# Column pieces for the gate and value products of the last three MLP steps of an attention-and-MLP kernel

## The chip, the cores and the metric

The kernel runs as one program on one core of a Trainium2 chip. The core has five engines that run their own instruction streams: TensorE (PE, with its weight loads shown apart as PEld), VectorE (DVE), ScalarE (ACT), GpSimd (POOL) and SyncE (SP, which only issues transfers). The metric is the device time of one execution in microseconds (us); lower is better. The median of three runs of the kernel before is 574.12 us.

## The reference

A gated linear recurrence over 768 tokens (4 batches, 8 heads of 48) gives `y`; its heads side by side are the 3072 x 384 input of a gated MLP with 1536 hidden units.

```python
for t in range(S):
    state = alpha[:, :, t, :, None] * state + np.einsum('bhd,bhe->bhde', k[:, :, t], v[:, :, t])
    y[:, :, t] = np.einsum('bhd,bhde->bhe', q[:, :, t], state)
...
g = x @ w_gate
silu = g * (1.0 / (1.0 + np.exp(-g)))
val = x @ w_val
return (silu * val @ w_out).astype(np.float32)
```

## The kernel before

The recurrence is done in 16 units of 192 tokens (chunks of 64), with short matmuls, scans and transposes. Their result, transposed and split in a high and a low part, is the tile `xT`: 128 partitions of features (three groups `kt` of 128) by 384 tokens. The MLP is done in 96 steps: 8 blocks of 384 tokens, and in each block 12 slices `f` of 128 hidden units. A step `s` has these instructions:

- `g{s}` on TensorE: the gate product, into one tile in PSUM (tag `gps`, one buffer). Operands are split in a high and a low part of type float32r, and three of the four products of parts are taken (`HL`), for each of three `kt`: nine pairs of a weight load of 128 columns and a matmul over 384 tokens, accumulated.
- `v{s}` on TensorE: the value product, in the same way (tag `vps`, one buffer).
- `sl{s}` on ScalarE: SiLU of the whole gate tile into `h`, one instruction; `h{s}` on VectorE: `h` times the whole value tile, one instruction.
- `hh{s}` on ScalarE and `hl{s}` on VectorE or GpSimd: the high part of `h`, and what is left.
- `o{s}` on TensorE: the output product, nine pairs as well, into three tiles `ops0` to `ops2` that gather over the steps of a block.

At the end of the last block, `ot95.0` to `ot95.2` copy the three output tiles on ScalarE, and `os95.0` to `os95.2` store them.

The order of all instructions on each engine is written out by hand in the string `ORDER` (`t` is TensorE, `v` VectorE, `s` ScalarE, `g` GpSimd, `y` SyncE); it holds for the whole main path. The end of it:

```python
... t:g92 s:hh91 t:v92 g:hl91 s:sl92 t:g93 v:h92 s:hh92 g:hl92 t:v93 s:sl93 t:g94 v:h93 t:v94
s:sl94 t:g95 v:h94 t:o91 t:o92 s:hh93 v:hl93 s:sl95 t:v95 s:hh94 g:hl94 t:o93 v:h95 t:o94 s:hh95
v:hl95 t:o95 s:ot95.0 s:ot95.1 y:os95.0 s:ot95.2 y:os95.1 s:os95.2
```

A small matmul `cps` (L931) of a range check stands in this stretch too, ahead of `g93`. Because each PSUM tag has one buffer, `g{s+1}` waits for `sl{s}`, and `v{s+1}` for `h{s}`. `product` (L720 and on) is what the change edits; L725 is its matmul, L757 the one of `out_product`. After the main path a flag decides whether a general path runs; with these inputs it does not.

Of the kernel before, what the change touches and what calls it, by code (L numbers as in the profile page):

```python
# [18 lines left out]
P = 128  # L19
# [3 lines left out]
NB = 384  # L23
# [15 lines left out]
LOW3 = 7.49 / 2.0 ** 32  # L39
F_LEAST = 3.4332275390625e-05  # L40
F_MOST = 122880.0

# [138 lines left out]
def main_path(ctx, tc, q, k, v, alpha, w_gate, w_val, w_out, out, flag, spill):  # L183
# [5 lines left out]
    nc = tc.nc  # L189
# [4 lines left out]
    KT = DM // P  # L194
    NF = DFF // P
# [89 lines left out]
    wsp, groups, wtiles = {}, [], []  # L285
# [84 lines left out]
    for x, t_ in enumerate(sels):  # L370
        nc.gpsimd.memset(t_.bitcast(F32), 0.0)
        for r in (0, BO):
            c0 = SEL + (D if (r > 0) != (x > 0) else 0)
# [302 lines left out]
    xT = {}  # L676
# [39 lines left out]
    HL = ((0, 0), (0, 1), (1, 0))  # L716
# [2 lines left out]

    def product(kind, blk, f):  # L720
        pt = acc[kind, blk, f] = ps.tile([P, NB], F32, tag=kind + "ps", name=f"{kind}{blk}_{f}")
        n = 0
        for kt in range(KT):
            for a, b_ in HL:
                nc.tensor.matmul(  # L725
                    pt, wsp[kind, f][a][:, kt * P : (kt + 1) * P], xT[blk][:, b_, kt, :],
                    start=(n == 0), stop=(n == 3 * KT - 1),
                )
                n += 1

    def silu(blk, f):
        h = acc["h", blk, f] = p2.tile([P, NB], F32, tag="h", name=f"h{blk}_{f}", bufs=NH)
# [150 lines left out]
    def named_step(s):  # L883
        blk, f, first, last = steps[s]
        b = (blk, f)
        todo[f"g{s}"] = lambda eng: product("g", *b)
        todo[f"sl{s}"] = lambda eng: silu(*b)
        todo[f"v{s}"] = lambda eng: product("v", *b)
        todo[f"h{s}"] = lambda eng: hidden(*b)
        todo[f"hh{s}"] = lambda eng: hidden_hi(*b)  # L890
        todo[f"hl{s}"] = lambda eng: hidden_lo(*b, eng)
        todo[f"o{s}"] = lambda eng: out_product(blk, f, first, last)
        for i in range(NTT):

            todo[f"pl{s}.{i}"] = lambda eng, i=i: part_load(blk, i)
            todo[f"ot{s}.{i}"] = lambda eng, i=i: out_rows(blk, f, i, eng)
            todo[f"os{s}.{i}"] = lambda eng, i=i: out_store(blk, f, i, eng)
# [38 lines left out]
def general_path(ctx, tc, q, k, v, alpha, w_gate, w_val, w_out, out, scratch):  # L936
# [73 lines left out]
    with tc.tile_pool(name="hp", bufs=2) as hp, tc.tile_pool(name="hps", bufs=1, space=PSUM) as hps:  # L1010

        def weights(dst, w, rows, cols):
# [8 lines left out]
            for step in single(nc, raw, t):  # L1021
# [7 lines left out]
            nc.vector.tensor_scalar(  # L1029
                out=m, in0=ab, scalar1=F_MOST, scalar2=3.0e38, op0=ALU.is_ge, op1=ALU.mult  # L1030
            )
# [84 lines left out]
```

## Time and profile before

| what | value |
|---|---|
| runs | 571.64, 574.12, 575.03 us; median 574.12 us |
| span of the profiled execution, first to last instruction | 570.8 us (its own device time is not listed apart from the runs; the fastest run is 0.8 us above the span, the median 3.3 us) |
| busy: PE, PEld, DVE, ACT, POOL | 545.7, 527.4, 391.7, 280.5, 134.0 us |
| stretch from the start of `g93` to the end of the last matmul | about 546.7 to 564.2 us |
| after the last matmul | about 6.6 us: one copy, one store |

A row of a timeline gives the start and the duration in us, then engine, line, operation, tiles and forms; `xN` at its end means that N instructions in a row are merged, from the start of the first to the end of the last. PE and PEld are pipelined: one matmul is shown as 0.34 us long while the next starts 0.17 us after it, so a pace is worked out from starts, not from durations.

### The profile page before, as it was taken

What the parts mean: (1) busy time and instruction counts of PE and PEld (TensorE: products, weight loads), DVE (VectorE), ACT (ScalarE), POOL (GpSimd) and SP (SyncE); (2) the same over time, 40 slices, a digit from 0 to 9 for tenths busy, and PEclk for the clock granted to TensorE, in tenths of its full rate; (3) what the DMA queues carried; (4) which work ended last, traced back from release to release, by engine and by line L of the source; (5) the groups of instructions that cost most, each with busy time, mean ns of one, the idle gap of its engine ahead of it and who ended that gap; (6) DMA issues with size and microseconds to landing.
All of it is one profiled execution on the core that took longest, in us unless ns stands there. A gap on an engine that the chain in (4) does not pass through costs nothing.

```text
span 570.8 us, 13758 instructions
## 1 busy us (share of the span) xinstructions
PE 545.7 (96%) x5510; PEld 527.4 (92%) x5510; DVE 391.7 (69%) x601; ACT 280.5 (49%) x621; POOL 134.0 (23%) x152
## 2 busy tenths in 40 slices
PE   4779999999999999999999999999999999999995
PEld 3669889999999999998999999999999999999995
DVE  6899998989989999889889698951793111210211
ACT  6778565325221223232224647675665666655712
POOL 4004513634431320341220022300131121012010
PEclk9989999999999999999999999999999999999998
DMA  7998934314555554554447667753742443324101
GB/s 204 309 318 254 277 82 112 115 40 108 131 146 146 135 132 107 124 126 113 93 100 187 172 156 205 191 141 89 218 111 85 116 132 86 97 73 121 41 2 47
DMA packets 95367, 77.66 MB, mean 136 GB/s; under 512 B 32832, under 2 KB 92224, under 8 KB 95296
## 3 DMA queue, kind: packets, MB, share of 16 engines
q1 hardware_dynamic: 95152, 76.51, 50.2%
q8 instruction: 45, 0.74, 0.6%
q14 instruction: 26, 0.21, 0.1%
q10 hardware_dynamic: 144, 0.20, 0.1%
HBM read 62.52 MB, written 5.90 MB: 120 GB/s over the span
## 4 chain that ended last, share of the span: by engine, by line
PE 76%; DMA 10%; DVE 7%; SPq 3%; issue 2%; ACT 1%; DVEq 0%; ACTq 0%
PE ops L757 24%; PE v L725 23%; PE g L725 22%; DMA raw<-in_moe_w_out_dram 3%; DMA raw<-in_moe_w_gate_dram 2%; PE y L652 2%; PE A L580 2%; PE s L556 2%; DMA raw<-in_moe_w_val_dram 1%; DMA L<-in_k_dram 1%; DMA Le<-in_q_dram 1%; DVE K L531 1%; SPq L436 1%; PE y L635 1%; DVE t L165 1%
## 5 line engine op out<-in xcount | busy, mean ns | idle before, releaser
L725 PE MATMUL v<-xT,w 128*128 128x384 f32 x864 | 166.9, 337 | 3.2 <-DVE h L737 2.4
L725 PE MATMUL g<-xT,w 128*128 128x384 f32 x864 | 167.3, 337 | 0.4 <-ACT h L733 0.4
L757 PE MATMUL ops<-w,hh 128*128 128x384 f32 x576 | 159.8, 338 | 0.0
L725 PEld LDWEIGHTS v<-xT,w 128*128 128x128 f32 x864 | 150.7, 188 | 5.8 <-DVE h L737 3.4
L725 PEld LDWEIGHTS g<-xT,w 128*128 128x128 f32 x864 | 150.7, 188 | 1.4 <-ACT h L733 0.7
L737 DVE TENSOR_TENSOR h<-h,v 128x384 f32<-128x384 f32 x96 | 52.9, 551 | 120.1 <-PE v L725 92.5
L746 POOL TENSOR_TENSOR hl<-h,hh 128x384 fp32r<-128x384 f32 x57 | 65.5, 1150 | 264.7 <-ACT hh L741 263.5
L741 ACT CAST hh<-h 128x384 fp32r<-128x384 f32 x96 | 49.1, 511 | 128.1 <-DVE h L737 70.9
L757 PEld LDWEIGHTS ops<-w,hh 128*128 128x128 f32 x576 | 105.5, 188 | 1.0
L757 PE MATMUL ops<-w,hl 128*128 128x384 f32 x288 | 96.8, 336 | 0.0
L733 ACT ACTIVATE h<-g 128x384 f32<-128x384 f32 x96 | 46.9, 489 | 80.6 <-PE g L725 68.8
L531 DVE STREAM_TRANSPOSE K<-Gs 32x384 f32<-32x384 f32 x96 | 54.7, 570 | 2.3 <-PE A L580 0.4
L757 PEld LDWEIGHTS ops<-w,hl 128*128 128x128 f32 x288 | 54.1, 188 | 0.1
L746 DVE TENSOR_TENSOR hl<-h,hh 128x384 fp32r<-128x384 f32 x39 | 22.9, 589 | 14.8 <-ACT hh L741 14.6
L590 DVE TENSOR_TENSOR X<-s,mask 64x384 f32<-64x384 f32 (+1 forms) x48 | 26.3, 552 | 8.5 <-PE s L556 7.6
L471 DVE TENSOR_TENSOR_SCAN AT<-AT,back 128x771 f32<-128x771 f32 x16 | 30.9, 1933 | 0.6
L462 DVE TENSOR_TENSOR_SCAN Gs<-AT,inj 128x772 f32<-128x772 f32 x16 | 28.7, 1794 | 0.1
L417 PE MATMUL pt<-ident,wide 128*128 128x128 f32 x72 | 14.9, 376 | 11.4 <-POOL mask L243 5.1
L417 PEld LDWEIGHTS pt<-ident,wide 128*128 128x128 f32 x72 | 12.1, 197 | 13.4 <-ACT wide L405 5.1
L319 ACT ACTIVATE wc<-wc,wbias 128x384 f32<-128x384 f32 x36 | 23.4, 650 | 1.2
L318 ACT ACTIVATE wc<-wc,wbias 128x384 f32<-128x384 f32 x36 | 23.3, 648 | 1.2
L839 POOL TENSOR_TENSOR Gs<-trk,Gs 128x768 f32<-128x768 f32 x10 | 17.9, 1785 | 25.3 <-DVE Gs L462 13.8
(118 smaller groups left out, 608.4 us busy)
## 6 DMA issues: line engine op xcount, KB each, us to landing
xT<-X SPq DMA_DIRECT2D x84, 72.0 KB, 2.2
raw<-in_moe_w_gate_dram SPq DMA_DIRECT2D x12, 384.0 KB, 7.5
V<-in_v_dram SPq DMA_DIRECT2D x96, 48.0 KB, 2.8
raw<-in_moe_w_val_dram SPq DMA_DIRECT2D x12, 384.0 KB, 7.9
raw<-in_moe_w_out_dram SPq DMA_DIRECT2D x12, 384.0 KB, 7.5
wc<-in_moe_w_gate_dram SPq DMA_DIRECT2D x12, 384.0 KB, 4.8
wc<-in_moe_w_val_dram SPq DMA_DIRECT2D x12, 384.0 KB, 3.5
wc<-in_moe_w_out_dram SPq DMA_DIRECT2D x12, 384.0 KB, 3.4
```

Of the source, the lines that this page charges most:

```text
L319: nc.scalar.activation(dev, dev, AF.Relu, bias=wbias[:, 1:2], accum_out=wviol[:, 0, i : i + 1])
L417: nc.tensor.transpose(pt[:, j - js.start, :], Wd.rearrange("p j e c -> p (j e c)")[:, j * P : (j + 1) * P], ident)
L462: nc.vector.tensor_tensor_scan(*(x.rearrange("p g t -> p (g t)")[:, ::-1] for x in (Gs, AT, inj)), 0.0, op0=ALU.mult, op1=ALU.add)
L471: nc.vector.tensor_tensor_scan(Af, Af, back[:, 1 : n + 1], back[:, 0:1], op0=ALU.mult, op1=ALU.add)
L531: nc.vector.transpose(out=bass.AP(k0.tensor, k0.offset, [k0.ap[0], (G * 2 * D, NU), (2 * D, G), (1, 32)]), in_=Kg[j * BO + x : j * BO + x ...
L590: nc.vector.tensor_tensor(out=X[r, z, f * GF : (f + 1) * GF, :].rearrange("r g (c t) -> r g c t", c=NU), in0=sps[f][r].rearrange("r g (c t ...
L725: nc.tensor.matmul(pt, wsp[kind, f][a][:, kt * P : (kt + 1) * P], xT[blk][:, b_, kt, :], start=(n == 0), stop=(n == 3 * KT - 1),)
L733: nc.scalar.activation(h, acc.pop(("g", blk, f)), AF.Silu)
L737: nc.vector.tensor_tensor(out=h, in0=h, in1=acc.pop(("v", blk, f)), op=ALU.mult)
L741: nc.scalar.copy(out=hh, in_=acc["h", blk, f])
L746: eng.tensor_tensor(out=hl, in0=acc.pop(("h", blk, f)), in1=hh.bitcast(F32), op=ALU.subtract)
L757: nc.tensor.matmul(ops[blk][i], h[b_][:, i * P : (i + 1) * P], wsp["o", f][a], start=(first and n == 0), stop=(last and n == 2),)
```

## The change

Steps 93, 94 and 95 (block 7, slices 9, 10 and 11) issue their gate and value products in two pieces of columns (tokens): 256 and 128, 320 and 64, 128 and 256. Each piece goes through all nine pairs of weights before the next piece starts, into its own columns of the same PSUM tile, and every pair loads its weights anew. SiLU, the product `h` and all that follows stay single instructions over 384 columns, and `ORDER` is the same.

```diff
+PARTS = {93: (0, 256, 384), 94: (0, 320, 384), 95: (0, 128, 384)}
...
     def product(kind, blk, f):
         pt = acc[kind, blk, f] = ps.tile([P, NB], F32, tag=kind + "ps", name=f"{kind}{blk}_{f}")
-        n = 0
-        for kt in range(KT):
-            for a, b_ in HL:
-                nc.tensor.matmul(
-                    pt, wsp[kind, f][a][:, kt * P : (kt + 1) * P], xT[blk][:, b_, kt, :],
-                    start=(n == 0), stop=(n == 3 * KT - 1),
-                )
-                n += 1
+        cuts = PARTS.get(blk * NF + f, (0, NB))
+        for c0, c1 in zip(cuts, cuts[1:]):
+            n = 0
+            for kt in range(KT):
+                for a, b_ in HL:
+                    nc.tensor.matmul(
+                        pt[:, c0:c1], wsp[kind, f][a][:, kt * P : (kt + 1) * P], xT[blk][:, b_, kt, c0:c1],
+                        start=(n == 0), stop=(n == 3 * KT - 1),
+                    )
+                    n += 1
```

TensorE before, from the range check's matmul to the first output product that follows (`g_9` is the gate tile of slice 9 in block 7, so of step 93; the last number of a name is its buffer's; each row of a product is nine pairs):

```order
L931 MATMUL cps<-oka,ones 1x1
L725 MATMUL g_9_6689<-xT_5746,w_1380 128x384 x9
L725 MATMUL v_9_6704<-xT_5746,w_1533 128x384 x9
L725 MATMUL g_10_6716<-xT_5746,w_1732 128x384 x9
L725 MATMUL v_10_6727<-xT_5746,w_1732 128x384 x9
L725 MATMUL g_11_6739<-xT_5746,w_1874 128x384 x9
L757 MATMUL ops_0_0_6462<-w_1380,hh_7_6673 128x384
```

The same place with the change (lines are four further down):

```order
L935 MATMUL cps<-oka,ones 1x1
L729 MATMUL g_9_6689<-xT_5746,w_1380 128x256 x9
L729 MATMUL g_9_6689<-xT_5746,w_1380 128x128 x9
L729 MATMUL v_9_6713<-xT_5746,w_1533 128x256 x9
L729 MATMUL v_9_6713<-xT_5746,w_1533 128x128 x9
L729 MATMUL g_10_6734<-xT_5746,w_1732 128x320 x9
L729 MATMUL g_10_6734<-xT_5746,w_1732 128x64 x9
L729 MATMUL v_10_6754<-xT_5746,w_1732 128x320 x9
L729 MATMUL v_10_6754<-xT_5746,w_1732 128x64 x9
L729 MATMUL g_11_6775<-xT_5746,w_1874 128x128 x9
L729 MATMUL g_11_6775<-xT_5746,w_1874 128x256 x9
L761 MATMUL ops_0_0_6462<-w_1380,hh_7_6673 128x384
```

Nothing has changed places; five rows of nine pairs have become ten. The last value product, `v95`, stands between the output products `o92` and `o93` on TensorE, before:

```order
L757 MATMUL ops_2_0_6464<-w_1533,hh_8_6700 128x384
L757 MATMUL ops_2_0_6464<-w_1533,hl_8_6702 128x384
L757 MATMUL ops_2_0_6464<-w_1533,hh_8_6700 128x384
L725 MATMUL v_11_6774<-xT_5746,w_1890 128x384 x9
L757 MATMUL ops_0_0_6462<-w_1874,hh_9_6768 128x384
```

and with the change:

```order
L761 MATMUL ops_2_0_6464<-w_1533,hh_8_6709 128x384
L761 MATMUL ops_2_0_6464<-w_1533,hl_8_6711 128x384
L761 MATMUL ops_2_0_6464<-w_1533,hh_8_6709 128x384
L729 MATMUL v_11_6819<-xT_5746,w_1890 128x128 x9
L729 MATMUL v_11_6819<-xT_5746,w_1890 128x256 x9
L761 MATMUL ops_0_0_6462<-w_1874,hh_9_6813 128x384
```

It has become two rows and stands where it stood. On the other four engines the main path has the same instructions in the same order. In all, 54 pairs of a weight load and a matmul of 384 columns have become 108 pairs of 64 to 320 columns.

## The prediction

> **What bounds the kernel now.** I read the page first: its busy table, its slices and its costliest groups.
>
> ```profile
> span 570.8 us, 13758 instructions
> ...
> PE 545.7 (96%) x5510; PEld 527.4 (92%) x5510; DVE 391.7 (69%) x601; ACT 280.5 (49%) x621; POOL 134.0 (23%) x152
> ...
> PEclk9989999999999999999999999999999999999998
> ...
> L725 PE MATMUL v<-xT,w 128*128 128x384 f32 x864 | 166.9, 337 | 3.2 <-DVE h L737 2.4
> L725 PE MATMUL g<-xT,w 128*128 128x384 f32 x864 | 167.3, 337 | 0.4 <-ACT h L733 0.4
> ```
>
> TensorE is busy for 96% of the span, and the two products that the change edits waited 3.2 and 0.4 us in the whole run. But a share over the span says little about the last 18 us, where the edit lies. So next the chain of work that ended last, asked for the end of the run only, and the busy time of that stretch:
>
> ```profile
> 546.65 0.12 PE cps L931 x2
> 546.76 1.77 PE g L725 x9
> 548.53 1.57 PE v L725 x9
> 550.11 1.57 PE g L725 x9
> 551.68 1.57 PE v L725 x9
> 553.25 1.57 PE g L725 x9
> 554.82 3.12 PE ops L757 x18
> 557.95 1.56 PE v L725 x9
> 559.50 4.70 PE ops L757 x27
> ...
> 564.28 0.48 ACT ot L769
> ```
>
> ```profile
> 546.60:564.20 17.60, 17.59 (x102) 17.24 (x101) 3.39 (x7) 4.42 (x9) 2.02 (x2) 1.00 0.01 3
> ```
>
> From `g93` at 546.76 to the last matmul at 564.2 us the chain is TensorE and nothing else: no other engine, no transfer. The columns of the second row are the window, its length, and the busy time of PE, PEld, DVE, ACT and POOL, then the granted clock (1.00: full) and the DMA share. PE and PEld fill the stretch, the other three are idle for three quarters of it or more. So any time that TensorE gains or loses in the six edited products goes to the end one to one.
>
> **What the six products cost now.** Five of the six pieces of the chain are 1.56 or 1.57 us for nine pairs, 0.174 us a pair; the first `g93` has 0.2 us more for what it waits behind the small `cps`, which stays. So 54 pairs cost 54 x 0.174 = 9.4 us.
>
> **What the change removes, adds and moves.** It removes 54 pairs of 384 columns and adds 54 pairs of the wider piece (36 of 256 columns, 18 of 320) and 54 of the narrower (36 of 128, 18 of 64). The columns are as many as before; the weight loads double. It moves nothing and adds no wait: the first matmul of a product waits for its PSUM tile as before, and SiLU and `h` wait for the last piece. The one-buffer PSUM tiles do not bind either:
>
> ```profile
> 548.63 0.49 ACT L733 ACTIVATE h<-g 128x384 f32<-128x384 f32 x1 [0.77 <-PE g L725]
> 549.77 1.59 PEld L725 LDWEIGHTS g<-xT,w 128*128 128x128 f32 x9
> 549.95 1.73 PE L725 MATMUL g<-xT,w 128*128 128x384 f32 x9
> ```
>
> SiLU of step 93 has emptied the gate tile at 549.12, and `g94` starts to fill it at 549.95 (its weights load from 549.77): 0.83 us of slack, and slower products widen it, since `v93` lies between them. Behind `v95` nothing is edited: `h95`, `hh95`, `hl95` and `o93` to `o95` follow its end as they do now. So the sum is one price list: what a pair costs at 256, 320, 128 and 64 columns. No row of this trace has a float32r product of that width, so I bound each from rows.
>
> *The wider pieces.* If a pair costs in proportion to its columns, 0.174 x 256/384 = 0.116 us and 0.174 x 320/384 = 0.145 us; the other end is that it does not shrink at all, 0.174. I take the proportional ends, provided that the weight load keeps up, which is the next question.
>
> *The narrower pieces.* In proportion these would be 0.058 and 0.029 us. A pair can't be faster than its weight load, and what that takes is hidden in the steady stream, where loads simply follow the matmuls. It shows where TensorE starts after a pause:
>
> ```profile
> 93.38 0.30 PEld L725 LDWEIGHTS v<-xT,w 128*128 128x128 f32 x2 [0.77 <-DVE h L737]
> 93.38 0.45 PE L725 MATMUL v<-xT,w 128*128 128x384 f32 x1 [0.45 <-DVE h L737]
> ...
> L725 PEld LDWEIGHTS g<-xT,w x864: 186/188/192, 51.6 to 554.3; 128*128 128x128 f32 x173
> L725 PE MATMUL g<-xT,w x864: 331/335/446, 51.7 to 554.5; 128*128 128x384 f32 x173
> ```
>
> The first row merges two loads: 0.30 us in all, of which the second takes its 0.188 (the row's median), so it started 0.11 us after the first, with nothing in front of it. The second row says the same by another road: the first matmul after the pause is shown as 0.45 us long where the median is 0.335, so it stood 0.11 us before its weights were in. I read both as the time to fill the array with 128 float32r columns: 0.11 us. That is less than the 0.116 of the 256-column piece, so loads stay hidden there, and more than what 128 or 64 columns take to stream. Loads are one ahead at most (in the rows of `g94` the first load starts 0.18 us, one pair, ahead of its matmul), so a run of nine narrow pairs goes at the pace of the loads: 0.11 us a pair at 128 columns and the same at 64. The bounds: 0.058 and 0.029 below, if loads somehow overlap each other; 0.22 above, if such narrow products are paid as full float32 ones (a rival below).
>
> **The sum.**
> - 256 and 128 columns (four products, 36 pairs of each): 0.116 + 0.110 - 0.174 = 0.052 us; x 36 = 1.9 us.
> - 320 and 64 columns (two products, 18 pairs of each): 0.145 + 0.110 - 0.174 = 0.081 us; x 18 = 1.5 us.
> - Together 3.4 us (3.33 before rounding), all on the path. Nothing covers it, and nothing comes back: the 6.6 us behind the last matmul are a copy and a store that don't change.
>
> The page's span of 570.8 becomes 574.2 us. The runs lie above their span (571.64 at the least, 574.12 in the median, 3.3 above this profiled one), so I add the 3.4 us to the median: 577.5 us, 0.6% slower.
>
> [...]
>
> **The rivals.**
>
> *Loads hidden, no loss (the other side: not slower).* If the weight loads of narrow pairs ran ahead by more than one, TensorE would only see columns, which are as many as before: 0 us, 574.1. It decides from the point where two loads overlap so far that a pair falls under 0.058 us. For it: a plain float32 load of the same 128 columns is spaced closer than float32r's, 0.20 - 0.14 = 0.06 us:
>
> ```profile
> 50.64 0.20 PEld L417 LDWEIGHTS pt<-ident,wide 128*128 128x128 f32 x2
> L417 PEld LDWEIGHTS pt<-ident,wide x72: 138/230/231, 5.0 to 51.1; 128*128 128x128 f32 x72
> ```
>
> Against it: that is another type, and the products themselves show 0.11. [...]
>
> *Narrow products paid as full float32.* The width might decide the mode: a float32r product too narrow might go as slowly as a float32 one. What that costs is in the trace:
>
> ```profile
> 20.65 0.82 PE L417 MATMUL pt<-ident,wide 128*128 128x128 f32 x6
> L417 PE MATMUL pt<-ident,wide x72: 271/421/477, 5.1 to 51.2; 128*128 128x128 f32 x72
> L556 PE MATMUL s<-X,Gs 48*64 48x64 f32 x768 | 15.4, 227 | 1.4 <-ACT K L520 1.4
> ```
>
> Six float32 passes over 128 columns start (0.82 - 0.27)/5 = 0.11 us apart, and a float32 product needs two passes: the code issues 16 x 24 = 384 score matmuls at L556, and the row has 768. So 0.22 us at 128 columns; at 64, two loads of 0.06 or two passes of 0.055, 0.12 us. Sum: 36 x (0.116 + 0.22 - 0.174) + 18 x (0.145 + 0.12 - 0.174) = 5.8 + 1.6 = 7.5 us, 581.6. Against it: the built program has one matmul for each pair of a narrow piece, as for a wide one (it has one for a float32 product too, though, so this says little). [...]
>
> *A flat price.* If 0.174 us were the cycle of a load and its matmul whatever the width (a load is shown as 0.188 us long), the 54 added pairs would cost 54 x 0.174 = 9.4 us: 583.5. Against it is the same 0.11 between loads.
>
> **How the numbers follow.** Narrow pairs at the pace of loads: 0.64, around 577.5 with its own range 575.5 to 579.5 (0.10 to 0.12 us a narrow pair moves it by 0.5 us each way, and the three runs before spread by 3.4 us). Paid as float32: 0.20, near 581.6. Hidden: 0.11, near 574.1 or, half way, 576. Flat: 0.05, near 583.5. The range 574.4 to 582.5 leaves out the flat price and half of the hidden case. About 0.5%, 2.9 us, is what a measurement of this kernel can tell from no change. The likeliest case is only just over that, so I give 0.43 of its 0.64 to slower and 0.21 to same; with 0.20 and 0.05 slower is 0.68, same is 0.21 and 0.09 of the hidden case, 0.30, and faster the rest, 0.02.
>
> **What would show it.** In the changed kernel's timeline, runs of nine pairs on PEld of the edited products: by my prices 1.04 us for 256 columns, 1.3 for 320 and 1.0 for both 128 and 64, from first start to the next piece's first start. Nine 64-column pairs as long as nine 128-column ones would show the loads as the limit; half as long, the columns; 128 at twice the length of 64, or x18 instead of x9, the float32 price; 1.57 for each, the flat price. TensorE should still have no wait in that stretch, and the chain should still be TensorE up to the last copy. I am wrong if loads speed up once matmuls are short, if a switch between widths costs something of its own, or if the median moves by its own spread.

## The result, and the profile after

The changed kernel takes 578.21 us in the median of 9 runs (576.82 to 580.04), the kernel before 573.08 us (9 runs, 571.64 to 575.03). The ratio is 1.0089 with a 95% interval of 1.0071 to 1.0107: 5.1 us slower, where 3.4 us were forecast. The profiled execution has a span of 575.1 us where before had 570.8; its own time was 576.82 us, so 1.7 us lie around a span.

The chain of work that ended last, for the end of the changed kernel's run (start, duration, what; lines are four further down than before):

```profile
547.06 0.12 PE cps L935 x2
547.18 2.21 PE g L729 x18
549.39 2.04 PE v L729 x18
551.43 2.30 PE g L729 x18
553.72 2.33 PE v L729 x18
556.05 2.13 PE g L729 x18
558.17 3.13 PE ops L761 x18
561.30 2.03 PE v L729 x18
563.34 4.70 PE ops L761 x27
...
568.11 0.48 ACT ot L773
```

Against the rows of before, the two products of step 93 went from 1.77 and 1.57 to 2.21 and 2.04, those of 94 from 1.57 and 1.57 to 2.30 and 2.33, those of 95 from 1.57 and 1.56 to 2.13 and 2.03. The sum is 9.61 before and 13.04 after: 3.4 us, and the chain from `g93` to the last matmul grew by as much, from 17.45 (546.76 to 564.21) to 20.85 us (547.18 to 568.03). Nothing else is in it. The busy times of that stretch say the same (window, length, then PE, PEld, DVE, ACT, POOL, granted clock):

```profile
547.05:568.03 20.98, 20.97 (x156) 20.62 (x155) 3.39 (x7) 4.42 (x9) 2.02 (x2) 1.00 0.01 2
```

DVE, ACT and POOL do to the hundredth what they did before, and wait for TensorE: in this window `h` on DVE waited 13.9 us in all for the value products, SiLU on ACT 5.1 us for the gate products, and `hl` on POOL 16.2 us for `hh` of ACT, which itself waited 8.6 us for output products. How a pair of each width is paced shows in the timeline of weight loads, cut inside one piece at a time. These are loads of the 64-column, the 128-column, the 320-column and the 256-column pieces, in this order:

```profile
552.75 0.86 PEld L729 LDWEIGHTS g<-xT,w 128*128 128x128 f32 x7
550.42 0.86 PEld L729 LDWEIGHTS v<-xT,w 128*128 128x128 f32 x7
551.61 0.92 PEld L729 LDWEIGHTS g<-xT,w 128*128 128x128 f32 x6
549.64 0.64 PEld L729 LDWEIGHTS v<-xT,w 128*128 128x128 f32 x5
```

With 0.188 us for the last load of each row, the spacing is (0.86 - 0.19)/6 = 0.112 us for 64 columns and the same for 128; 0.92 gives 0.146 for 320, 0.64 gives 0.113 for 256. Half the columns are no faster: the loads set the pace there. At 256 columns the price by columns (0.116) and the load (0.112) lie too close together to tell which of them sets it.

So 3.4 us of the 5.1 are as forecast, and some 1.7 us lie elsewhere. In this profile 0.4 us lie ahead of `g93` (547.18 against 546.76), and another place shows at once: the copy that ends the chain starts 6.5 us before the end of the span before (564.28 of 570.8) and 7.0 us after (568.11 of 575.1). What SyncE waited for there, before and then after (engine and line, releaser: total, times, longest):

```profile
SPq L1084 <- SPq L1084: 3.4, 1, 3.4
```

```profile
SPq L1088 <- SPq L1088: 4.8, 2, 2.9
```

L1084 (now L1088) is the branch around the general path. SyncE stood still on nothing but itself, once before and twice after, in the closing instructions that follow the jump. The page's row on queue 14 has one more transfer of instructions, before and then after:

```profile
q14 instruction: 26, 0.21, 0.1%
```

```profile
q14 instruction: 27, 0.22, 0.1%
```

In the trace's records the second pause is 1.8 us long, from 571.65 to 573.48 us. The view of transfers in just that window has two packets, both on queue 14 (one more, on queue 8, where the page counts 46 and before 45, starts just ahead of that window, at 571.62 us, and takes 0.9 us); in the kernel before two run as well behind its one pause (568.9 to 570.8 us), and SyncE goes on through them. The changed kernel first, then the kernel before:

```profile
q14 instruction: 2, 0.02, 2.8%
```

```profile
q14 instruction: 2, 0.02, 3.2%
```

The 27th transfer starts behind the second pause, at 574.1 us. A wait for data is ruled out: the instruction behind the pause waits for a semaphore that a transfer last raised at 522.1 us (521 to 531 us in the nine profiles below and here that have such a pause).

### The profile page after: what moved, and what is told of

Read it like the earlier page. It is cut to its first block, busy times and chain, and to the rows that moved or that the text cites. A ratio compares the mean times of both kernels' runs of the same rounds, so it can differ in the third digit from the quotient of the medians.

```text
span 575.1 us, 13866 instructions
## 1 busy us (share of the span) xinstructions
PE 545.7 (95%) x5564; PEld 527.6 (92%) x5564; DVE 391.6 (68%) x601; ACT 280.5 (49%) x621; POOL 133.1 (23%) x152
## 4 chain that ended last, share of the span: by engine, by line
PE 77%; DMA 8%; DVE 7%; SPq 4%; issue 2%; ACT 1%; POOL 0%; DVEq 0%; ACTq 0%; POOLq 0%
PE ops L761 23%; PE v L729 23%; PE g L729 22%; DMA L<-in_alpha_dram 2%; PE A L582 2%; PE y L654 2%; PE s L558 2%; SPq L711 2%; DMA raw<-in_moe_w_val_dram 1%; DMA L<-in_k_dram 1%; DMA V<-in_v_dram 1%; PE y L637 1%; PE y L638 1%; DVE K L533 1%; DMA Le<-in_q_dram 1%
## 5 line engine op out<-in xcount | busy, mean ns | idle before, releaser
L729 PE MATMUL v<-xT,w 128*128 128x384 f32 (+3 forms) x891 | 168.5, 333 | 4.5 <-DVE h L741 3.6
L729 PE MATMUL g<-xT,w 128*128 128x384 f32 (+3 forms) x891 | 169.0, 334 | 0.4 <-ACT h L737 0.4
L729 PEld LDWEIGHTS v<-xT,w 128*128 128x128 f32 x891 | 152.7, 188 | 6.8 <-DVE h L741 4.3
L729 PEld LDWEIGHTS g<-xT,w 128*128 128x128 f32 x891 | 152.7, 188 | 1.4 <-ACT h L737 0.7
L419 PE MATMUL pt<-ident,wide 128*128 128x128 f32 x72 | 12.4, 327 | 12.2 <-POOL mask L245 5.1
L419 PEld LDWEIGHTS pt<-ident,wide 128*128 128x128 f32 x72 | 9.9, 168 | 14.0 <-ACT wide L407 5.1
```

Source lines behind the costliest of these rows:

```text
L729: nc.tensor.matmul(pt[:, c0:c1], wsp[kind, f][a][:, kt * P : (kt + 1) * P], xT[blk][:, b_, kt, c0:c1], start=(n == 0), stop=(n == 3 * KT - 1),
```

## The experiments

Two questions: whether it is the loads that price a narrow pair, and what the rest of the loss is. In the accounts, "stretch" is from the chain's first `g93` row to the end of its last output product (17.45 before), and "closing" from the start of the chain's last copy to the end of the span (6.5 us before); the expectations count the closing from the last matmul's start, 0.4 us more. All kernels ran in five rounds beside the kernel before.

**The kernel before, again** (no edit).

> The kernel before, against itself. If the 1.7 us by which the measured loss (5.1 us) exceeds what TensorE's chain lost in the trace (3.4 us) is scatter between executions, two sets of runs of one kernel differ by something of that order, and this ratio lies between 0.998 and 1.002 with an interval of about 0.2% each way. A second profile also shows how far the start of g93 (546.7 us) and the end behind the last matmul (6.6 us) move by themselves: by 0.5 us or more if they are scatter, by under 0.1 us if the 0.4 and 0.5 us seen there belong to the change.

Ratio 0.9996 (0.9980 to 1.0012). Its `cps` ran 0.5 us later than in the first profile, but the stretch and the closing are the same: 564.80 of 571.3, 6.5 us, with one self-wait of 3.2 us. So the 0.4 us ahead of `g93` is within scatter, and the closing hardly moves. That scatter is wide: in the profiles below without an edit ahead of it, `g93` starts anywhere from 546.4 to 550.2 us. Totals are therefore compared by medians, and the closing by its own rows.

**The changed kernel, again** (no edit).

> The changed kernel once more. Loads as the limit: from g93 to the last matmul again 20.85 us in the trace where before had 17.44. The total: 1.006 to 1.007 if only TensorE's 3.4 to 3.9 us count and the first measurement was high by scatter; 1.009 again if there is a constant loss of 1.2 to 1.7 us beside the chain.

Ratio 1.0112 (1.0088 to 1.0136). The stretch is as in the first profile, and the closing is 8.5 us, 567.42 of 575.9. SyncE's waits:

```profile
SPq L1088 <- SPq L1088: 5.2, 2, 3.4
```

The second pause costs 1.8 us (5.2 - 3.4). In the first profile most of it was hidden: SyncE issued its two last stores in 0.85 us, where the kernel before took 1.66, and the first pause was 2.9 us instead of 3.4, together 1.3 us less. Its stores before, and then after:

```profile
563.69 1.66 SPq L774 DMA_DIRECT2D out_dram<-ot  x2
```

```profile
567.52 0.85 SPq L778 DMA_DIRECT2D out_dram<-ot  x2
```

There is a constant loss beside the chain. By the ratio it would be 3.0 us here (6.4 of 573.0, less 3.4), more than the pause; the interval reaches down to 1.6, and whether the rest is more than scatter is not shown.

**The pieces in the middle of the run.**

```diff
-PARTS = {93: (0, 256, 384), 94: (0, 320, 384), 95: (0, 128, 384)}
+PARTS = {57: (0, 256, 384), 58: (0, 320, 384), 59: (0, 128, 384)}
```

> The same pieces in steps 57 to 59, some 220 us from the end, instead of 93 to 95. Loads as the limit: each product's pace is as in steps 93 to 95, the six products lose 3.4 us, and since TensorE waits nowhere for more than 0.5 us after 267 us, the total loses the same 3.4 us (1.006). A loss that belongs to the end of the program (its last instructions, their fetch) would not be there: total 1.006 where the changed kernel has 1.009. If other engines' waits absorb it in the middle, under 1.004.

Ratio 1.0095 (1.0067 to 1.0122). The edited products in the chain:

```profile
369.73 1.98 PE g L729 x18
371.70 1.63 PE ops L761 x9
373.34 1.97 PE v L729 x18
375.31 2.29 PE g L729 x18
377.61 1.67 PE ops L761 x9
379.27 2.24 PE v L729 x18
...
384.98 2.04 PE g L729 x18
387.02 2.07 PE v L729 x18
```

The six take 12.59 us, 3.2 us more than six products of 1.56; the two output products behind narrow pieces take 0.16 us more than the usual 1.57 each, which makes 3.4. The stretch at the end is as in the kernel before (551.84 to 569.28 us, 17.44). So nothing absorbed the loss later, and the place in the run does not matter. The total did not drop to 1.006, and the closing, where nothing was edited, is 9.1 us (569.36 of 578.5):

```profile
SPq L1088 <- SPq L1088: 6.2, 2, 4.2
```

The constant loss has no need of an edit near the end.

**Pieces that alternate within each pair of weights.**

```diff
-        for c0, c1 in zip(cuts, cuts[1:]):
-            n = 0
-            for kt in range(KT):
-                for a, b_ in HL:
+        n = 0
+        for kt in range(KT):
+            for a, b_ in HL:
+                for c0, c1 in zip(cuts, cuts[1:]):
...
-                        start=(n == 0), stop=(n == 3 * KT - 1),
+                        start=(n == 0 and c0 == 0), stop=(n == 3 * KT - 1 and c1 == NB),
...
-                    n += 1
+                n += 1
```

> Same pieces and steps, but the two pieces alternate within each pair of weights (256, 128, 256, 128, ...) instead of nine of one and nine of the other: 17 changes of width in a product instead of 1. Loads as the limit, each one ahead at most: a pair still costs the longer of its columns and the next load, 0.116 + 0.112, so the stretch loses 3.4 us again. A cost of the change of width: 17 times that of one, well over 10 us. Loads that can run further ahead: the wide matmuls hide part of the narrow ones' loads, and the stretch loses under 2 us.

Ratio 1.0120 (1.0089 to 1.0151). The stretch is 20.97 us (546.52 to 567.49), 3.5 us more than before, so seventeen changes of width cost hardly more than one (20.85). Whether loads run further ahead only the products of 320 and 64 columns can tell: 18 loads of 0.112 are 2.02 us, about what a product of 256 and 128 columns takes either way. By those loads alone all six products would lose 2.7 us, so the "under 2 us" of the expectation was too low. The two products of step 94:

```profile
550.78 2.30 PE g L729 x18
553.08 2.34 PE v L729 x18
```

They stay at the 2.32 us of nine times 0.146 + 0.112, not 2.02: a wide matmul does not hide the load after next, and no more than one load ahead shows here. The ratio is 3.4 us above the stretch, with an interval down to 1.6; what of it is not the second pause is again not shown.

**Halves, 320 and 64 everywhere, thirds.**

```diff
-PARTS = {93: (0, 256, 384), 94: (0, 320, 384), 95: (0, 128, 384)}
+PARTS = {s: (0, 192, 384) for s in (93, 94, 95)}         # halves
+PARTS = {s: (0, 320, 384) for s in (93, 94, 95)}         # 320 and 64
+PARTS = {s: (0, 128, 256, 384) for s in (93, 94, 95)}    # thirds
```

> Pieces of 192 and 192 columns in all six products, the same 54 added pairs. Loads as the limit: 192 columns would stream in 0.087 us, under the 0.112 of a load, so both pieces go at 0.112: 18 x 0.112 = 2.02 us a product where 1.57 was, the stretch loses 2.7 us. A flat cost of each added pair (3.4 us / 54 = 0.064): 3.4 us. Columns as the limit: 0.

> Pieces of 320 and 64 columns in all six products, again 54 added pairs. Loads as the limit: 0.147 + 0.112 - 0.174 = 0.085 us a pair, the stretch loses 4.6 us: more than with halves, though as many pairs are added and as many columns streamed. A flat cost of each added pair: 3.4 us.

> Three pieces of 128 columns in all six products, 108 added pairs. Loads as the limit: 27 x 0.112 = 3.02 us a product, the stretch loses 54 x (0.336 - 0.174) = 8.7 us. A flat cost of each added pair: 108 x 0.064 = 6.9 us. Columns as the limit: 0. If there is a constant loss of 1.2 to 1.7 us beside the chain, the total loses that much more than the stretch here too.

The first two products of step 93 and the last output products in the chains of these three kernels, in the same order:

```profile
546.79 2.19 PE g L729 x18
548.97 2.01 PE v L729 x18
...
562.14 4.72 PE ops L761 x27
```

```profile
546.39 2.44 PE g L729 x18
548.83 2.32 PE v L729 x18
...
563.60 4.78 PE ops L761 x27
```

```profile
550.19 3.16 PE g L729 x27
553.35 3.01 PE v L729 x27
...
571.55 4.75 PE ops L761 x27
```

In the table, the flat price is 0.064 us for each added pair, which the changed kernel itself gives (3.4 us over 54).

| kernel | added pairs | stretch, us | more than before | by loads | by a flat price | ratio (95%) |
|---|---|---|---|---|---|---|
| halves | 54 | 20.07 | 2.6 | 2.7 | 3.4 | 1.0066 (1.0044 to 1.0089) |
| changed | 54 | 20.85 | 3.4 | 3.4 | 3.4 | 1.0089 (1.0071 to 1.0107) |
| 320 and 64 | 54 | 21.99 | 4.5 | 4.6 | 3.4 | 1.0120 (1.0087 to 1.0153) |
| thirds | 108 | 26.11 | 8.7 | 8.7 | 6.9 | 1.0178 (1.0142 to 1.0213) |

With the same columns and the same number of added pairs, halves lose 2.6 us and skewed pieces 4.5. That tells the price of loads from a price per pair, and both from a price per column, which would be 0 for all. Every ratio is again above its stretch, by 1.2 us (halves) to 2.3 us (320 and 64), and each of the three new kernels has the second pause, of 1.6 to 1.8 us.

**More instructions, products as before.** Twenty-seven float32 matmuls of one column, first on TensorE.

```diff
+    def more_code(eng):
+        dm = ps.tile([1, 1], F32, tag="ops2", name="dm")
+        for _ in range(27):
+            nc.tensor.matmul(dm, back[:, 0:1], back[:, 1:2], start=True, stop=True)
...
-ORDER = """
+ORDER = """
+t:dm
```

> The products as before; 27 float32 matmuls of one column (54 pairs of a load and a matmul, as many instructions as the change adds) at TensorE's start, where it waits until 5 us anyway. Their result is not used. If the loss beside the chain comes from 108 more instructions in TensorE's program (their fetch, or where the later ones lie), the total loses 1 to 1.7 us with g93 to the last matmul at 17.4 us; if that loss was scatter, 1.000 within 0.2%.

Ratio 1.0026 (1.0008 to 1.0045): slower by 1.5 us. The closing is 8.3 us (565.51 of 573.8), with a second pause of 1.7 us:

```profile
SPq L1090 <- SPq L1090: 5.2, 2, 3.5
```

(The page counts 28 transfers of instructions here; the one more than in the changed kernel starts at 0.2 us, so it is not of the closing.) So the constant loss comes without any piece. The records place the second pause behind the 4th of SyncE's closing instructions (changed kernel, pieces that alternate), behind the 5th (mid-run, halves, more instructions) or the 6th (320 and 64, thirds). In the built programs SyncE has 1286 instructions where the pause is behind the 4th, 1285 for the 5th, 1284 for the 6th, and 1290 in the kernel before: count and place add up to 1290 each time. Its main path is the same in all of them (the trace has 746 of its instructions in every run); by the built programs, what differs is how many waits the scheduler gave it in the general path, which stands ahead of the closing instructions and is jumped over. That makes a theory, so far an assumption of the author: SyncE fetches its program in pieces, a border between two of them lies at a fixed distance from the program's start, and in the kernel before the closing instructions begin just at it. The rival is that anything added costs it.

**The border moved, three ways.** Small transfers at the head of the general path, which does not run; the main path is untouched on all engines.

```diff
+    for i in range(4):   # changed kernel: 1293 on SyncE; before: range(2), 1286, and range(8), 1292
+        nc.sync.dma_start(out=scratch[i : i + 1, 0:D], in_=q[0, 0, i : i + 1, :])
     hot = cp.tile([P, 2 * D], F32, name="hot")
```

> The changed kernel with four small transfers added to the general path, which does not run; the main path is the same. SyncE's program has 1293 instructions by count of the built program instead of 1286 (the kernel before: 1290). If the pause of 1.8 us in SyncE's closing instructions stands where its code crosses from one fetched piece of code to the next, it moves with the count (after the 4th at 1286, the 5th at 1285, the 6th at 1284) and at 1293 lies before the closing ones: no second pause, 6.9 us from the last matmul's start to the end as in the kernel before, the total 1.006 (3.4 us of TensorE alone). If more instructions in themselves cost it, 8.7 us and 1.009 to 1.011 as before.

> The kernel before, with two small transfers added to the general path, which does not run; the main path is the same on all engines. SyncE's program has 1286 instructions instead of 1290 (the scheduler arranges the general path with fewer waits). A crossing between pieces of code: a pause of 1.8 us after the 4th closing instruction, as in the changed kernel, 8.7 us from the last matmul's start to the end, the total 1.003. If the loss belongs to TensorE's added instructions: no pause, 6.9 us, 1.000.

> The kernel before, with eight small transfers added to the general path, which does not run: 1292 instructions on SyncE. A crossing between pieces of code: it lies before the closing instructions, no second pause, 6.9 us and 1.000 within 0.2%, although more has been added than in the run with two. If anything added to the general path costs time: 1.003 or more.

SyncE's waits on itself in the three, in that order, and the page's row on queue 14 of the second and third (the first has 26 too):

```profile
SPq L1090 <- SPq L1090: 3.0, 1, 3.0
```

```profile
SPq L1086 <- SPq L1086: 5.2, 2, 3.3
...
q14 instruction: 27, 0.22, 0.1%
```

```profile
SPq L1086 <- SPq L1086: 3.3, 1, 3.3
...
q14 instruction: 26, 0.21, 0.1%
```

| kernel | SyncE's instructions | second pause | closing, us | ratio to before (95%) |
|---|---|---|---|---|
| changed, four transfers | 1293 | none | 6.2 | 1.0058 (1.0035 to 1.0081) |
| before, two transfers | 1286 | 1.9 us, behind the 4th | 8.3 | 1.0024 (1.0007 to 1.0041) |
| before, eight transfers | 1292 | none | 6.6 | 1.0003 (0.9981 to 1.0025) |

Each came out as the border has it and against the rival: two transfers cost 1.4 us, eight cost nothing, and four give the changed kernel 1.8 us back, so that it loses 3.3 us, the 3.4 us of TensorE's chain. The ratios alone would be weak evidence, since their intervals overlap (1.0058 with the changed kernel's first 1.0089, and 1.0024 with 1.0003); the second pause, there or gone as forecast, and the transfer on queue 14 that comes and goes with it carry the argument. A border that costs a fetch agrees with these rows; no row shows the fetch itself, and the size of a piece was not measured here.

No version tried is faster than the kernel before. The pieces only add loads, and by this theory that kernel's closing instructions already lie at the start of a fetched piece.

## Why the prediction was right or wrong

The measured time of 578.2 us lies in the range and went the way forecast, with the mechanism that was forecast for TensorE. That it lies so close to the 577.5 is in part luck: the forecast started from the median of three runs, 574.12 us, and nine gave 573.08, so a base 1.0 us too high made up for more than half of the 1.7 us that were missing in the loss. That the kernel came out clearly slower owes something to luck too: TensorE's loss alone, as the changed kernel with four transfers shows it (1.0058), is only just over the 0.5% that the prediction could tell from no change. By its steps:

- *Any time that TensorE gains or loses goes to the end one to one.* Right: the six products and the chain both grew by 3.4 us, and in the middle of the run the products and what follows them lost as much.
- *Wider pieces in proportion to their columns.* Right within 0.003 us: 0.113 to 0.118 for 256 columns (0.116), 0.146 for 320 (0.145).
- *Narrow pieces at the pace of loads, 0.11 us at 128 and 64 columns.* Right: 0.112 for both. The 0.11 us between two loads after a pause was the pace of a load, and the 0.188 us of a load's row was not.
- *The sum, 3.4 us on TensorE.* Right: 3.40 us.
- *"Nothing comes back: the 6.6 us behind the last matmul are a copy and a store that don't change."* Here the prediction failed. The copy and the store did not change, but SyncE's closing instructions lie in those 6.6 us too, and a second pause of 1.8 us came into them. That term was set to 0. It was not in the list of what moves, because only the main path was compared: the general path, which does not run, had been arranged anew, and SyncE's program had become four instructions shorter. 3.4 + 1.8 = 5.2 us stand against the measured 5.1.
- The rivals. *Loads hidden* fell: pairs of 128 columns went at 0.112 us, not 0.058. *Paid as float32* fell: 64 and 128 columns cost the same, 0.112 us and not 0.12 and 0.22. *A flat price* fell: 0.112 instead of 0.174.
- *Nine pairs take 1.04, 1.3 and 1.0 us at 256, 320 and both narrow widths.* Right. In the loads of `v93` and `g94` they take 1.03 us at 256, 1.28 at 320, 1.01 at 128 and 1.04 at 64 columns, and a whole product of the chain takes 2.03 to 2.33 us, where the prices give 2.03 and 2.30 (`g93` at 2.21 still has its 0.2 us behind `cps`, and `g95` at 2.13 follows a 64-column piece).

## What to carry to other kernels

In this kernel a run of matmuls with a new load each had the pace of the slower of two things, its columns (0.146 us a pair at 320) and its weight load (0.112 us at 192, 128 and 64). The load's pace could be read beforehand behind a pause, from the distance of the second load to the first (0.11 us). As an estimate from 0.112 us a load and 0.174 us for 384 columns, about 250 float32r columns are the least that keeps TensorE at the pace of its columns; cutting columns below that cost time even though the columns stayed as many (2.6 us with halves of 192). And a change of one or two microseconds can come from code that never runs (1.4 us from two transfers in the general path): compare where the closing instructions of each engine wait (here one pause of 3.4 us or two of 3.3 and 1.9), and how many instruction transfers the page counts (26 or 27 on queue 14), before a small loss is put down to the edit.

## What the runs showed of the hardware

- SyncE stood still for 2.9 to 4.2 us after its jump over the general path, and in nine of the thirteen profiles for another 1.6 to 2.0 us a few instructions later. The place of that second pause moved by one instruction for each that its program was longer or shorter (1284 to 1286).
- The load of 128 float32r columns had a pace of 0.112 us beside matmuls of 64, 128 and 192 columns alike (18 of them took 2.01 us in a product of halves), and 0.11 behind a pause with nothing in front, at 93.38 us of the kernel before. That is about twice the 0.06 us between two float32 loads of as many columns, read at one transpose (L417, at 50.64 us).
- The count and place of SyncE's instructions are from the built programs and the trace's records; that the pause is a fetch is concluded from its place, from the extra transfer on queue 14 and from the three shifted kernels. Which address the border has, and for which engine a transfer on queue 8 or 14 is, was not read.
